# Both heads of an attention unit turned on VectorE, scores made two steps ahead, and a reordered last batch, in a fused top-k attention and feed-forward kernel

## The chip, the cores and the metric

The kernel runs on one core of a Trainium2 chip. A core has five engines that run their own instruction streams [...]: TensorE (PE in the profile, with its weight loads shown apart as PEld), VectorE (DVE), ScalarE (ACT), GpSimd (POOL) and SyncE (SP), which here only issues DMAs. The metric is device time in microseconds (us) for one whole execution; lower is better.

## The reference

Two blocks in sequence, all in float32. With batch B = 8, H = 8 heads, S = 576 rows and head width D = 64:

```
scores = (1/8) * q @ k^T                        # per batch and head, 576 x 576
kth    = 32nd largest score of each row
scores = where(scores >= kth, scores, -1e9)
attn   = exp(scores - max) / (sum + 1e-9)
x      = (attn @ v), heads side by side         # B x S x 512
xn     = (x - mean) / sqrt(var + 1e-6) * g_ln   # per row
out    = x + relu(xn @ w_ch1) @ w_ch2           # 512 -> 2048 -> 512
```

## The kernel before

**Units, groups, jobs.** The 576 query rows of a head are cut into four full blocks of 128 rows and a rest of 64. A *unit* is one block for a pair of heads: a full unit holds the two heads as two tiles of 128 x 576 scores; a rest unit packs the 64 rest rows of both heads into one tile. A *group* is a set of units of one head pair whose probabilities are multiplied with the values together (blocks 0 and 1, or 2 and 3, with the rest rows, J = 4, put with one of them). A *job* is a group's work with its loads. There are 5 units for each of 4 head pairs and 8 batches: 160 units, in `units`, batch by batch.

**The step loop** (L900) makes one pass per unit and six more. In step n it works on several units at once, and the order of the calls in the loop is the order of the instructions on every engine; nothing is rescheduled. For unit n, `select` finds the 32nd largest score on VectorE, in four parts spread over the step. For unit n+1, `scores` (L329) makes the scores on TensorE, and ScalarE copies them from PSUM to a tile `sc`. For unit n-1, `mask` (L439) forms a masked score on ScalarE; for unit n-2, called `ex`, `weigh` (L446) takes the exponential with its row sum on ScalarE, and the probabilities are turned so that keys lie on partitions. For the group that ended at unit n-3, `values` (L558) multiplies the turned probabilities, in the tile `pt`, with v. `place` turns the result back and scales it by the row sums.

**Select.** From the ninth unit on, `halve` (L363) first folds a row of 576 into its larger and its smaller halves: VectorE writes `hi` = max(a, b), and GpSimd writes `lo` = a + b, and then lo - hi, in whole numbers. `select_halved` (L381) takes the 16 largest of `lo`, puts them behind `hi`, and then takes the 32 largest of 304 by MAX8 and MATCH_REPLACE8. The first eight units use 576-wide MAX8 and MATCH_REPLACE8 on `sc` instead (L416, L423).

**Turning.** For most tiles, `turn` (L496) turns on TensorE: four 128 x 128 transposes per head (L505), one more for the ends of both heads (L538), and ScalarE copies to `pt`. From batch 2 on, units that are not a group's last and not rest units are *moved* (72 of them): `move` (L478) turns their second head with one VectorE transpose of 32 x 32 blocks into the unit's own `sc`, SyncE stores that to HBM, and four DMAs bring it back to `pt` with the blocks in place. `move` comes after the first part of `select` in the step, and that unit's second head is masked and weighed first (`order`, L914).

**Feed-forward.** When the rows of a block of two or three 128-row tiles are complete (`gives`), its work is queued in `todo`: turn x, first products ("hidden", L680, four per 128 hidden columns), second products ("project", L697). `fill`, called at eight places in a step, takes from that list as much as `slot(n)` allots, so TensorE works on it between attention instructions. `slot` spreads the list evenly over the steps up to the next block.

**Weights.** The weights come as float64; in the first steps `Piece.split`, `shift` and `join` make float32 of them on ScalarE, VectorE and GpSimd. The gain g_ln is multiplied into w_ch1 on GpSimd in `join`.

**Buffers that matter here:** `sc` has 4 tiles, `e` (masked scores, then probabilities) 2, `lo` 1, `pt` 1, five PSUM banks serve scores, turns and values, and three serve the feed-forward products.

Of the kernel before, what the change touches and what calls it, by code (L numbers as in the profile page):

```python
# [16 lines left out]
TOP_K = 32  # L17
# [12 lines left out]
def kernel(  # L30
# [66 lines left out]
    scpool = pool("sc", 4)  # L97
# [4 lines left out]
    otpool = pool("ot", 2)  # L102
# [4 lines left out]
    rpool = pool("r", 2)  # L107
# [34 lines left out]
    class Piece:  # L142
# [26 lines left out]
        def split(self):  # L169
# [5 lines left out]
            self.low = tmp("low", FP32)  # L175

            pl, tag = ((opool, "o"), (rpool, "r"))[self.i % 2]
            self.sign = pl.tile([P, DM], FP32, tag=tag, name="sign")
# [5 lines left out]
            nc.scalar.activation(self.sign[:], high, AF.Sign)  # L184
            nc.gpsimd.tensor_scalar(size_f, size_f, HIGH_MAX, HIGH_MIN, ALU.min, ALU.max)
# [6 lines left out]
        def join(self):  # L192
            size = self.size[:]
            nc.gpsimd.tensor_tensor(size, size, self.low[:].bitcast(U32), ALU.add)
            size = size.bitcast(FP32)
            if self.i < NF:
                gain = gcol[:, self.c : self.c + 1].to_broadcast([P, DM])
                nc.gpsimd.tensor_tensor(size, size, gain, ALU.mult)
            nc.gpsimd.tensor_tensor(self.dst, size, self.sign[:], ALU.mult)
            ready[self.i] = now[0]  # L200
# [107 lines left out]
    class Unit:  # L308
        def __init__(self, job, group, qt):
# [5 lines left out]

            self.halved = False
# [46 lines left out]
    def halve(u):  # L363
# [11 lines left out]
        nc.gpsimd.tensor_tensor(lo.bitcast(I32), a.bitcast(I32), b.bitcast(I32), ALU.add)  # L375
        nc.vector.tensor_tensor(hi, a, b, ALU.max)  # L376
        nc.gpsimd.tensor_tensor(  # L377
            lo.bitcast(I32), lo.bitcast(I32), hi.bitcast(I32), ALU.subtract
        )

    def select_halved(u, i):  # L381
# [24 lines left out]
    def select(u, i):  # L406

        if u.halved:
            return select_halved(u, i)
        nt = range(len(u.tiles))  # L410
        if i == 0:
            u.cur = [u.sc[:, t] for t in nt]
            u.wk = {}
        m = small.tile([P, 2, 8], FP32, tag=f"m{i}", name=f"m{i}")
        for t in nt:
            nc.vector.max(m[:, t, :], u.cur[t])  # L416
        if i < TOP_K // 8 - 1:
            for t in nt:
                if i == 0:

                    o = (NF - 4 + 2 * t) * DM
                    u.wk[t] = w2[:].rearrange("p f n -> p (f n)")[:, o : o + S]
                nc.vector.match_replace(u.wk[t], m[:, t, :], u.cur[t], LOWEST)  # L423
                u.cur[t] = u.wk[t]
        if i == 0:
            u.top = m
        u.thr = m

    def prepare(u):
# [5 lines left out]
        engine = nc.vector if u.i < CONVERTING else nc.gpsimd  # L435
        engine.tensor_tensor(b, u.thr[:, 0:nt, 7], u.top[:, 0:nt, 0], ALU.subtract)  # L436
        engine.tensor_scalar(b, b, scale, 0.0, ALU.mult, ALU.add)  # L437
# [28 lines left out]
    def place_of(u):  # L466
# [4 lines left out]
        if g.pt is None:  # L471
            g.pt = ptpool.tile([P, 2 * J + 1, GQ], FP32, tag="pt", name="pt")
            g.ptB = g.pt[:, J : 2 * J].rearrange("p c n -> p (c n)").rearrange(
                "p (i c n) -> p i c n", c=J, n=32
            )
        return sum(P for x in g.qts if x < u.qt)

    def move(u):  # L478

        i0 = place_of(u) // 32  # L480
        t = u.sc[:, 1, 0:JP]
        nc.vector.transpose(
            t.rearrange("p (j c n) -> p j c n", j=P // 32, c=J),
            u.e[:, 1, R:S].rearrange("p (c j k) -> p j c k", c=J, k=32),
        )
        hbm = hbmpool.tile([P, JP], FP32, tag="turned", name="turned")
        nc.sync.dma_start(hbm[:], t)
        for j in range(P // 32):
            nc.sync.dma_start(
                u.group.ptB[j * 32 : (j + 1) * 32, i0 : i0 + P // 32].rearrange(  # L490
                    "k i c n -> k i (c n)"
                ),
                hbm[:, j * P : (j + 1) * P].rearrange("(i k) x -> k i x", k=32),
            )

    def turn(u):  # L496

        g = u.group
        q0 = place_of(u)
        i0 = q0 // 32  # L500

        def part(t):
# [6 lines left out]
            if u.rest:  # L509
                both = ps[:].rearrange("p (c h n) -> p h c n", h=2, n=R)  # L510
                nc.scalar.copy(g.pt[:, 0:J, q0 : q0 + R], both[:, 0])
                nc.scalar.copy(
                    g.ptB[:, i0 : i0 + R // 32],
                    both[:, 1].rearrange("p c (i n) -> p i c n", n=32),
                )
            elif t == 0:
                nc.scalar.copy(  # L517
                    g.pt[:, 0:J, q0 : q0 + P], ps[:].rearrange("p (c n) -> p c n", n=P)
                )
            else:  # L520
                nc.scalar.copy(
                    g.ptB[:, i0 : i0 + P // 32],
# [18 lines left out]
        heads = [0] if u.moved else range(len(u.tiles))  # L541
# [16 lines left out]
    def values(g):  # L558
        vb = g.job.v
        av = brief("av")  # L560
        for c in range(J):
            for h in range(2):
# [3 lines left out]
                    g.ptB[:, 0 : g.nq // 32, c, :] if h else g.pt[:, c, 0 : g.nq],  # L566
# [47 lines left out]
    class Block:  # L614
# [40 lines left out]
        def items(self):  # L655
# [21 lines left out]
            def hidden(f, c):  # L677
                if c == 0:
                    ps["h"] = product("hps")
                nc.tensor.matmul(  # L680
                    ps["h"][:, 0:N],
# [5 lines left out]
                if c == NC - 1:  # L687
                    per = J // n if n in (1, 2) else 1
                    if f % per == 0:
                        hT["h"] = hpool.tile([P, J * P], FP32, tag="h", name="h")  # L690
                    hT[f] = hT["h"][:, f % per * N : (f % per + 1) * N]
                    nc.scalar.activation(hT[f], ps["h"][:, 0:N], AF.Relu)  # L692
# [363 lines left out]
```

## Time and profile before

| | |
|---|---|
| median of 3 runs | 1665.12 us (1665.03 to 1666.29) |
| the profiled execution | 1668.59 us, of which the span of its instructions 1666.8 us |
| TensorE matmul busy | 1574.1 us, 94% |
| VectorE busy | 1464.5 us, 88% |
| ScalarE busy | 1077.2 us, 65% |
| GpSimd busy | 664.0 us, 40% |
| DMA | 104.58 MB, mean 63 GB/s |

Engines overlap, so the shares do not add up to the span. A busy share is an average over the whole span; the start, the long middle and the end have different limits, and the page's slices show them apart. Float32 products appear in the trace as two matmul instructions each, transposes as one, so 576 second products of the program are 1152 in the profile. The end of a matmul is modelled; the distance from one start to the next is what a matmul takes in a run of them.

### The profile page before, as it was taken

What the parts mean: (1) busy time and instruction counts of PE and PEld (TensorE: products, weight loads), DVE (VectorE), ACT (ScalarE), POOL (GpSimd) and SP (SyncE); (2) the same over time, 40 slices, a digit from 0 to 9 for tenths busy, and PEclk for the clock granted to TensorE, in tenths of its full rate; (3) what the DMA queues carried; (4) which work ended last, traced back from release to release, by engine and by line L of the source; (5) the groups of instructions that cost most, each with busy time, mean ns of one, the idle gap of its engine ahead of it and who ended that gap; (6) DMA issues with size and microseconds to landing.
All of it is one profiled execution on the core that took longest, in us unless ns stands there. A gap on an engine that the chain in (4) does not pass through costs nothing.

```text
span 1666.8 us, 25284 instructions
## 1 busy us (share of the span) xinstructions
PE 1574.1 (94%) x7113; PEld 955.1 (57%) x7113; DVE 1464.5 (88%) x4476; ACT 1077.2 (65%) x2759; POOL 664.0 (40%) x879
## 2 busy tenths in 40 slices
PE   3568989989999999999999999999999999999998
PEld 1346556566555575755547575745547575755564
DVE  5998999999999999999999999899998999998000
ACT  5677967767666776767666675767666676665310
POOL 5567854343433434343343434343243433333010
PEclk9758999999999999999999999999999999999999
DMA  7423333001331133213231233112331132111000
GB/s 176 100 64 108 89 58 59 22 14 27 76 81 51 53 76 81 65 54 69 59 86 51 55 73 83 52 54 70 65 89 44 53 81 74 52 46 47 26 13 13
DMA packets 301203, 104.58 MB, mean 63 GB/s; under 512 B 246276, under 2 KB 283144, under 8 KB 301064
## 3 DMA queue, kind: packets, MB, share of 16 engines
q1 hardware_dynamic: 296328, 102.39, 24.4%
q10 hardware_dynamic: 4736, 0.59, 0.3%
q8 instruction: 57, 0.93, 0.2%
q14 instruction: 82, 0.67, 0.1%
HBM read 74.58 MB, written 28.31 MB: 62 GB/s over the span
## 4 chain that ended last, share of the span: by engine, by line
PE 71%; DVE 21%; issue 4%; ACT 2%; POOL 1%; DMA 1%; ACTq 0%; POOLq 0%; DVEq 0%; SPq 0%
PE hps L680 25%; PE ops L697 24%; PE scps L354 8%; PE av L563 6%; DVE m L398 5%; DVE hi L385 4%; PE tp L505 4%; DVE hi L390 2%; DVE m L416 2%; PE av L570 2%; DVE w L423 2%; DVE lo L385 1%; DVE hi L376 1%; DVE size L188 1%; PE tp L667 1%
## 5 line engine op out<-in xcount | busy, mean ns | idle before, releaser
L680 PE MATMUL hps<-xT,w 128*128 128x256 f32 (+1 forms) x2048 | 550.0, 411 | 2.7 <-ACT xT L672 2.3
L697 PE MATMUL ops<-w,h 128*128 128x512 f32 x1152 | 546.1, 599 | 0.0
L398 DVE MAX8 m<-hi 128x8 f32<-128x304 f32 x1088 | 460.7, 458 | 2.3
L680 PEld LDWEIGHTS hps<-xT,w 128*128 128x128 f32 x2048 | 372.1, 191 | 108.5 <-issue 17.3
L385 DVE MATCH_REPLACE8 hi<-m,hi 128x304 f32<-128x304 f32 x816 | 368.0, 456 | 0.0
L375 POOL TENSOR_TENSOR lo<-sc 128x576 int32<-128x576 int32 (+1 forms) x152 | 197.7, 1301 | 316.3 <-ACT sc L335 156.9
L697 PEld LDWEIGHTS ops<-w,h 128*128 128x128 f32 x1152 | 200.2, 191 | 169.9 <-issue 164.6
L377 POOL TENSOR_TENSOR lo<-lo,hi 128x576 int32<-128x576 int32 (+1 forms) x152 | 196.8, 1295 | 141.9 <-DVE hi L376 139.7
L354 PE MATMUL scps<-kT,qT 64*128 64x288 f32 (+3 forms) x1344 | 217.4, 433 | 32.4 <-DVE qT L304 20.9
L335 ACT COPY sc<-scps 128x288 f32<-128x288 f32 x576 | 199.2, 409 | 62.3 <-PE scps L354 51.0
L442 ACT ACTIVATE e<-sc,m 128x576 f32<-128x576 f32 x288 | 224.3, 779 | 9.7 <-DVE m L398 6.2
L452 ACT ACTIVATE e<-e,bias 128x576 f32<-128x576 f32 x288 | 224.6, 780 | 2.9 <-DVE bias L437 2.5
L390 DVE MAX8 hi<-lo 128x8 f32<-128x288 f32 x544 | 221.8, 443 | 2.6 <-POOL lo L377 1.5
L354 PEld LDWEIGHTS scps<-kT,qT 64*128 64x128 f32 (+1 forms) x1344 | 122.4, 181 | 146.6 <-issue 56.2
L505 PEld LDWEIGHTS tp<-ident,e 128*128 128x128 f32 x864 | 110.9, 147 | 115.9 <-ACT e L452 51.7
L505 PE MATMUL tp<-ident,e 128*128 128x128 f32 x864 | 138.1, 285 | 38.2 <-ACT e L452 37.9
L692 ACT ACTIVATE h<-hps 128x256 f32<-128x256 f32 (+1 forms) x256 | 105.9, 414 | 96.5 <-PE hps L680 93.8
L436 POOL TENSOR_TENSOR bias<-m,m 128x2 f32<-128x2 f32 (+1 forms) x143 | 27.8, 195 | 303.6 <-DVE m L398 303.6
L563 PE MATMUL av<-pt,vb 128*64 128x256 f32 (+2 forms) x1088 | 146.7, 413 | 0.0
L376 DVE TENSOR_TENSOR hi<-sc 128x576 f32<-128x576 f32 (+1 forms) x152 | 138.8, 913 | 5.5 <-ACT sc L335 5.5
L385 DVE MATCH_REPLACE8 lo<-hi,lo 128x288 f32<-128x288 f32 x272 | 118.2, 440 | 0.0
L517 ACT COPY pt<-tp 128x512 f32<-128x512 f32 x128 | 74.6, 583 | 62.1 <-PE tp L505 60.5
(79 smaller groups left out, 1295.0 us busy)
## 6 DMA issues: line engine op xcount, KB each, us to landing
turned<-sc SPq DMA_DIRECT2D x72, 256.0 KB, 2.0
pt<-turned SPq DMA_DIRECT2D x288, 64.0 KB, 2.0
vb<-in_v_dram SPq DMA_DIRECT2D x136, 128.0 KB, 2.5
raw<-in_moe_w_ch_dram SPq DMA_DIRECT2D x32, 512.0 KB, 4.0
kin<-in_k_dram SPq DMA_DIRECT2D x128, 72.0 KB, 2.5
qin<-in_q_dram SPq DMA_DIRECT2D x120, 72.0 KB, 2.5
out_dram<-o SPq DMA_DIRECT2D x32, 256.0 KB, 2.2
ends<-in_v_dram SPq DMA_DIRECT2D x136, 16.0 KB, 2.2
```

What stands on the lines that cost most here:

```text
L335: nc.scalar.copy(u.sc[:, t, s * HALF : (s + 1) * HALF], made[s][t][:, 0:HALF])
L354: nc.tensor.matmul(ps[i * R : i * R + ql, o : o + width], qT[r, q0 : q0 + ql], kT[r, k0 : k0 + width], start=True, stop=True,)
L375: nc.gpsimd.tensor_tensor(lo.bitcast(I32), a.bitcast(I32), b.bitcast(I32), ALU.add)
L385: nc.vector.match_replace(x[:, t], m[:, t, :], x[:, t], LOWEST)
L390: nc.vector.max(u.hi[:, t, o : o + 8], u.lo[:, t])
L398: nc.vector.max(m[:, t, :], u.hi[:, t])
L442: nc.scalar.activation(u.e[:, t], u.sc[:, t], AF.Prelu, bias=u.thr[:, t, 7:8], scale=-1.0, alpha=SLOPE)
L452: nc.scalar.activation(u.e[:, t], u.e[:, t], AF.Exp, bias=u.bias[:, t : t + 1], scale=-scale / SLOPE, accum_out=g.den[:, col : col + 1],)
L505: nc.tensor.transpose(ps[:, c * P : (c + 1) * P], u.e[:, t, c * P + t * R : (c + 1) * P + t * R], ident[:],)
L563: nc.tensor.matmul(av[h * D : (h + 1) * D, 0 : g.nq], vb[:, h * J + c, :], g.ptB[:, 0 : g.nq // 32, c, :] if h else g.pt[:, c, 0 : g.nq], ...
L680: nc.tensor.matmul(ps["h"][:, 0:N], w1[:, c, f * P : (f + 1) * P], xT[0][:, c, 0:N], start=(c == 0), stop=(c == NC - 1),)
L697: nc.tensor.matmul(ps[i][:], hT[f][:, i * P : (i + 1) * P], w2[:, f, :], start=(f == 0), stop=(f == NF - 1),)
```

## The change

It has these parts.

- **Turning.** A moved unit has both heads turned on VectorE (two transposes), one store of twice the size and four returning DMAs of twice the size. TensorE and ScalarE no longer turn its first head. `pt` holds both heads in blocks of 32 queries. `move` stands at the end of the step, after the last part of `select`, and the heads are masked and weighed in their natural order.
- **Scores two steps ahead.** From step 17 (`CONVERTING`) on, step n makes the scores of unit n+2 in place of n+1 (`due`). `sc` has five tiles in place of four; `ot` and `r` have one each in place of two.
- **Halving.** All units are halved, the first eight too. VectorE writes `hi` first; GpSimd then makes lo = a - hi, and lo + b.
- **Feed-forward.** For blocks of one or two tiles, the first products of four or two f share one PSUM bank, with one relu over 512 columns.
- **Last batch.** Its rest rows come first, as four groups of their own; then blocks 0 and 1, then 2 and 3. The last batch thus gives blocks of 1, 2 and 2 tiles in place of 3 and 2, and has 8 moved units in place of 12: 68 in all.
- **Weights.** The gain is multiplied into the sign on ScalarE in place of GpSimd; the sign's temporary is in another pool. The bias of the first units is one VectorE instruction per head.
- **Order in a step.** `values` stands after two fills, `stats` and the reciprocals later. `slot` shares the list out in proportion to VectorE's estimated time of each step (`pace`), not evenly.

```diff
-    scpool = pool("sc", 4)
+    scpool = pool("sc", 5)
-    otpool = pool("ot", 2)
+    otpool = pool("ot", 1)
-    rpool = pool("r", 2)
+    rpool = pool("r", 1)
...
             nc.scalar.activation(self.sign[:], high, AF.Sign)
+            if self.i < NF:
+                nc.scalar.mul(self.sign[:], self.sign[:], gcol[:, self.c : self.c + 1])
...
-            if self.i < NF:
-                gain = gcol[:, self.c : self.c + 1].to_broadcast([P, DM])
-                nc.gpsimd.tensor_tensor(size, size, gain, ALU.mult)
...
-        nc.gpsimd.tensor_tensor(lo.bitcast(I32), a.bitcast(I32), b.bitcast(I32), ALU.add)
         nc.vector.tensor_tensor(hi, a, b, ALU.max)
         nc.gpsimd.tensor_tensor(
-            lo.bitcast(I32), lo.bitcast(I32), hi.bitcast(I32), ALU.subtract
+            lo.bitcast(I32), a.bitcast(I32), hi.bitcast(I32), ALU.subtract
         )
+        nc.gpsimd.tensor_tensor(lo.bitcast(I32), lo.bitcast(I32), b.bitcast(I32), ALU.add)
...
     def move(u):
-        t = u.sc[:, 1, 0:JP]
-        nc.vector.transpose(
-            t.rearrange("p (j c n) -> p j c n", j=P // 32, c=J),
-            u.e[:, 1, R:S].rearrange("p (c j k) -> p j c k", c=J, k=32),
-        )
-        hbm = hbmpool.tile([P, JP], FP32, tag="turned", name="turned")
-        nc.sync.dma_start(hbm[:], t)
+        blocks = u.sc[:].rearrange("p t n -> p (t n)")[:, 0 : 2 * JP]
+        for t in range(2):
+            nc.vector.transpose(
+                blocks.rearrange("p (j t c n) -> p j t c n", j=ni, t=2, c=J)[:, :, t],
+                u.e[:, t, t * R : t * R + JP].rearrange("p (c j k) -> p j c k", c=J, k=32),
+            )
+        hbm = hbmpool.tile([P, 2 * JP], FP32, tag="turned", name="turned")
+        nc.sync.dma_start(hbm[:], blocks)
...
-        heads = [0] if u.moved else range(len(u.tiles))
+        heads = () if u.moved else range(len(u.tiles))
...
-                if c == 0:
+                per = J // n if n in (1, 2) else 1
+                o = f % per * N
+                if c == 0 and o == 0:
                     ps["h"] = product("hps")
...
+                if c == NC - 1 and f % per == per - 1:
+                    h = hpool.tile([P, J * P], FP32, tag="h", name="h")
...
+                    nc.scalar.activation(h[:, 0 : per * N], ps["h"][:, 0 : per * N], AF.Relu)
...
-            parts[b < 2].append(J)
+            if b == B - 1:
+                parts = [[J]] + parts
+            else:
+                parts[b < 2].append(J)
...
-    for u in units[EARLY:]:
-        u.halved = True
...
-    RESERVE = 4.0
+    RESERVE = 7.0
...
+    def due(n):
+        ahead = [n + 1] if n < CONVERTING else [n + 2]
+        if n == CONVERTING:
+            ahead = [n + 1, n + 2]
+        return [units[i] for i in ahead if i < N]
...
-        if nxt:
-            scores(nxt)
-        if g:
-            values(g)
+        for x in due(n):
+            scores(x)
         if u:
             select(u, 0)
-        if moved:
-            move(ex)
...
         fill()
+        if g:
+            values(g)
...
         if u:
             select(u, 3)
             if u.i < CONVERTING:
                 prepare(u)
+        if moved:
+            move(ex)
```

## The prediction

> **What bounds the kernel now.** I read the busy shares and the slices first, then the busy time of the long middle, the waits, the groups by shape, and the timeline of single steps.
>
> ```profile
> PE 1574.1 (94%) x7113; PEld 955.1 (57%) x7113; DVE 1464.5 (88%) x4476; ACT 1077.2 (65%) x2759; POOL 664.0 (40%) x879
> ...
> PE   3568989989999999999999999999999999999998
> PEld 1346556566555575755547575745547575755564
> DVE  5998999999999999999999999899998999998000
> ```
>
> A slice is 41.7 us. VectorE is full from the second slice on while TensorE is not, up to slice 9; then both are full; VectorE has nothing in the last three.
>
> ```profile
> 400.00:1500.00 1100.00, 1095.98 (x5004) 656.16 (x5000) 1053.08 (x3288) 735.92 (x1914) 419.09 (x598) 1.00 0.25 64
> ```
>
> Busy time between 400 and 1500 us: TensorE 99.6%, VectorE 95.7%. From some 400 us on TensorE sets the end; VectorE has 47 us to spare in 1100. In the waits, VectorE's idleness has one main name:
>
> ```profile
> DVE sc L482 <- ACT e L452: 59.4, 19, 13.4
> ```
>
> `move` waits for an exponential on ScalarE, which lags with TensorE: 19 waits, 59.4 us. Early, TensorE's first product starts at 132.30 us; before, it waits for steps paced by VectorE's select. So the early 130 us count by VectorE and the rest by TensorE.
>
> **What the Trainium skill says.** "SBUF — State Buffer" (section "SBUF: two separate sides"): a VectorE instruction with two SBUF inputs and a GpSimd instruction that reads SBUF lock each other out for the whole instruction. The trace agrees: the same `hi` takes 0.74 us alone and 1.92 us when GpSimd's L375 had begun just before.
>
> ```profile
> 913.84 0.74 DVE L376 TENSOR_TENSOR hi<-sc 128x576 f32<-128x576 f32 x1
> ...
> 922.37 1.41 POOL L375 TENSOR_TENSOR lo<-sc 128x576 int32<-128x576 int32 x1 [3.18 <-ACT sc L335]
> 922.47 1.92 DVE L376 TENSOR_TENSOR hi<-sc 128x576 f32<-128x576 f32 x1
> ```
>
> "DMA: Bandwidth & Descriptors" (section "Anatomy of one DMA — SWDGE (gpsimd) path") gives some 2 us fixed for a DMA through GpSimd; these go through SyncE, and still the page's section 6 shows 2.0 us for the 256 KB store and for the 64 KB returns.
>
> **The change, part by part.** Durations are of the profiled execution: span 1666.8 us, 1668.6 us as timed, the median 1665.1; I add on the span and take off 1.7 us at the end.
>
> *TensorE.* The programs' counts of L505 go from 864 to 608: 256 turns fewer (68 moved units without 8 turns, before 72 without 4). Their price is the start-to-start distance:
>
> ```profile
> 147.63 0.60 PE L505 MATMUL tp<-ident,e 128*128 128x128 f32 x4
> 148.07 1.25 PE L680 MATMUL hps<-xT,w 128*128 128x256 f32 x5
> ```
>
> Four take 0.44 us, so 256/4 x 0.44 = **-28.2 us** where TensorE is full. (The mean of 285 ns overlaps its neighbours.) ScalarE loses 64 copies of 0.58 us, hidden.
>
> The last batch's block of 3 tiles becomes 2 and 1. 64 products of 384 columns (2 x 0.323 us) become 64 of 256 (2 x 0.216) and 64 of 128. No row shows 128 columns: by columns 2 x 0.108, no loss; if the weight load's 191 ns binds, 2 x 0.191, +10.6 us. I take the middle, **+5**. Four value products for rest rows alone are about 1 us each (the first batch has them), less some 0.5 us for each narrowed group: **+2**.
>
> *VectorE.* Transposes go from 72 to 136: 64 x 0.698 = +44.7 us. `hi` now runs before GpSimd's two instructions, no longer during the first: 120 x (1.038 - 0.745) = -35 us. In the early units, by start-to-start distances in the timeline up to 125 us, a pair of 576-wide MAX8 takes 1.33 us and a pair of replaces 1.44, so 4 x 1.33 + 3 x 1.44 = 9.6; the halved way is 0.67 (`hi`) + 2 x 0.73 (MAX8 of `lo`) + 0.85 (its replaces) + 4 x 0.75 + 3 x 0.88 (MAX8 and replaces of `hi`) = 8.6. With some 0.5 us off the bias, -1.5 x 8 = -12 us. VectorE's sum is about -2, and the 59.4 us of waiting at `move` have a step's length more of cover.
>
> *Early.* Of those 12 us I keep **-8** for the start: the first select waits for `lo`, some 3.5 us (0.75 + 2 x 1.4) at one time; ScalarE gets 16 more activations of 0.68 us, 11 us, in a stretch where it is 76% busy (38.17 of 50 us), covered unless its step outgrows VectorE's; GpSimd loses 16 x 1.04 us and gains 8 x 2.8. Bounds: -16 (with most of the contention before 400 us, 4 us, added) and +4 (ScalarE takes over the pace).
>
> *`lo` later.* It is ready 2 x 1.43 = 2.9 us after `hi`, 1.4 later than now. Between stand select's parts 2 and 3, 1.6 + 2.4 us, so it is hidden in a full step. In a rest step they are 2.0 us with 1.4 of `move`: nothing to 0.9 us in 32 steps, absorbed by VectorE's slack. Both GpSimd instructions now wait for `hi`; behind them in GpSimd's queue stand the centring of x, the residual sum and the next bias, which TensorE's turn of x and ScalarE's exponential need a step or more later. Ahead of them stands at times a residual sum (1.29 us) that waits for the last second product; if TensorE lags far, that holds `lo`, and VectorE waits for TensorE there in place of at `move`.
>
> *`move` at the end of the step.* SyncE issues as many DMAs per unit. 512 KB stores: with 102 MB taking 24.4% of 16 engines' span, 256 KB more is about 1 us of all engines, so 2.0 to 3.0 us to land; total DMA share at most some 8 points more. On SyncE's queue `move` now stands behind the loads of heads and values; the values need `pt` more than a step later, so nothing. `sc` matters: in step n the copies of scores n+2 take the tile of unit n-3, which `move` read at the end of step n-1. Two transposes 1.4 us, issue 0.35, landing 2.1: free 3.8 us after that step's select ends. Queued behind that wait on ScalarE are relu, exponential and copies, and TensorE for their banks. I take **0**, since TensorE has a fill or two, the values and three product banks to go on with, and a constant lag is paid once. Below zero is not excluded: idle before VectorE's waits could shorten.
>
> *Hidden edits.* One relu per bank spares ScalarE instructions, and it idles 364 of the 1100 us; if its first product per bank now comes later, two other banks of the three cover 8 x 0.216 = 1.7 us each. `slot` and the later `values` move work between steps, 0 while TensorE is full. `ot` with one tile: its reader comes in the same step, and the next group a step later at least. In the last batch four head loads come in four steps; the first load of all took 4.4 us (2.32 to 6.75 in the chain), a step 5 or more: 0, at most 2 us three times, within VectorE's slack.
>
> Sum: 1666.8 - 28.2 + 5 + 2 - 8 = 1637.6 span, less 1.7: **1636 us**.
>
> Can VectorE keep up? After its last select at about 1536 TensorE had backlog until 1604. The least behind it is the last block (1604.67 to the end, 62 us) plus a drain of some 15 (masks and exponentials 3.5, turn 2, values and copies 5, statistics and centring 2, a fill). Its last select may end as late as 1638 - 77 = 1561. From 392 on it needs 1088 + 45 - 31 = 1102 of the 1169 us: 67 us of idleness are free.
>
> **Rivals.**
>
> *VectorE becomes the bound.* In a rest step (5 us of select) `move` needs the exponential, which came 4.6 us after the step's start before (913.64 against 909.00); with ScalarE lagging 3 us, VectorE waits about 2.5 us, 20 times, 50 us; with 0.9 x 32 for `lo`, 79. That passes the 67 by 12, and coupling may double it: 1648 to 1660, say 1654. For it: both engines are over 95% busy. Against: `pace` gives rest steps less TensorE work.
>
> *Slower: the `sc` wait holds TensorE.* Its scores at 909.00 and VectorE's next select (L390 at 909.26) start together now; so aligned, each of 68 moved units would hold ScalarE some 3 us. It decides once more than 31/68 = 0.45 us of each reaches TensorE; at 1 us: 1636 + 68 = 1704. Against: VectorE leads in those 19 waits, and a lag once taken covers the wait.
>
> *The gain is spent early or in the tail.* If the start gains nothing and 128-wide products cost +10.6: 1636 + 8 + 6 = 1650.
>
> *Better:* early -16, the narrow block free, and 1100 to 1500 stays full: 1636 - 8 - 5 - some = 1620.
>
> **How the numbers follow.** Within 0.2% (1661.8 to 1668.4) is what a measurement can hardly tell from no change. Likeliest, 1624 to 1648: 0.55. Better, under 1624: 0.12. VectorE bound or gain spent, 1648 to 1662: 0.17. About the same: 0.05. Slower, the `sc` wait: 0.11. The range 1618 to 1662 leaves out the slower case, half of the same, and the best few in a hundred. Faster 0.84, same 0.05, slower 0.11.
>
> **What would show it.** L505's successor x608; `hi` at a mean near 0.75 us; VectorE at 96% in the middle with TensorE still over 99%; the first product before 128 us; the wait of the transposes in `move` well under 59 us. Wrong: TensorE's scores or turns waiting on ScalarE's copies to `sc` by tens of us; VectorE waiting on GpSimd's `lo`; first products of 128 columns at 0.19 us each.

## The result and the profile after

The changed kernel takes **1674.64 us** (median of 4 runs, 1672.19 to 1675.20) against 1665.17 us before (1665.03 to 1666.29): a ratio of the means of 1.0053, 95% interval 1.0035 to 1.0070. It is slower by about half a per cent; the forecast was 1636 us with a range of 1618 to 1662. The profiled execution of the changed kernel took 1674.27 us, its span 1672.5 us.

The page of the changed kernel, busy time and slices (41.8 us each):

```profile
PE 1569.3 (94%) x7057; PEld 941.9 (56%) x7057; DVE 1469.6 (88%) x4611; ACT 1038.1 (62%) x2615; POOL 670.7 (40%) x881
...
PE   2568989989799999999999999999999999999998
...
DVE  5997999999989999999999999999889887988600
```

TensorE's busy sum fell by only 4.8 us where 28 us of turns went. There is a new dent, a 7 in slice 11 (418 to 460 us). The long middle of the changed kernel (columns: stretch, length, then busy time of TensorE, its weight loads, VectorE, ScalarE and GpSimd, the clock, the DMA share and GB/s):

```profile
400.00:1500.00 1100.00, 1083.99 (x4788) 630.90 (x4787) 1034.25 (x3252) 672.71 (x1743) 411.81 (x587) 1.00 0.34 92
```

TensorE idles 16 us of these 1100, before 4. VectorE is not fuller than before (1034 against 1053). The groups by shape, changed kernel:

```profile
L375 DVE TENSOR_TENSOR hi<-sc 128x576 f32<-128x576 f32 x128 | 99.1, 774 | 19.5 <-ACT sc L335 19.5
L468 DVE STREAM_TRANSPOSE sc<-e 128x512 f32<-128x512 f32 x136 | 89.5, 688 | 42.1 <-ACT e L436 42.0
L490 PE MATMUL tp<-ident,e 128*128 128x128 f32 x608 | 96.8, 284 | 26.4 <-ACT e L436 25.5
L193 DVE TENSOR_SCALAR size<-size 128x512 uint32<-128x512 uint32 x32 | 30.7, 997 | 0.0
```

The 256 turns are gone (x608), `hi` has a mean of 774 ns in place of 1038, the second transposes are there. The last line is a surprise, taken up at the end. The waits of the changed kernel (total us, times, longest):

```profile
DVE sc L468 <- ACT e L436: 42.0, 20, 6.9
DVE hi L391 <- POOL lo L379: 34.2, 17, 7.5
...
DVE hi L375 <- ACT sc L335: 21.4, 9, 7.2
...
ACT sign L187 <- POOL w L201: 15.0, 7, 2.9
...
ACT sc L335 <- DMA turned<-sc: 10.7, 4, 4.9
```

`move` waits less than before (59.4 us then). VectorE's wait for `lo` was 1.5 us, once, before. Its longest in the changed kernel, with GpSimd's instructions ahead of it (a square bracket is the idle time before the instruction and what ended it):

```profile
1392.18 1.27 POOL L693 TENSOR_TENSOR o<-o,x 128x512 f32<-128x512 f32 x1 [16.78 <-ACT o L689]
1393.41 0.79 POOL L376 TENSOR_TENSOR lo<-sc,hi 128x288 int32<-128x288 int32 x1
...
1395.12 0.46 DVE L391 MAX8 hi<-lo 128x8 f32<-128x288 f32 x1 [7.53 <-POOL lo L379]
```

A residual sum on GpSimd has waited for ScalarE's `o`, which follows TensorE's last second product, and `lo` stands behind it. Nine of the 17 waits, 26.6 of the 34.2 us, follow such a held sum. ScalarE's wait for GpSimd's `w` at `sign`, 6.0 us in 3 times before, is 15.0 us in 7. The last line is the `sc` wait of the slower rival: 10.7 us in 4 times, not 68 times 3 us. DMA issues and their landing, changed kernel:

```profile
turned<-sc SPq DMA_DIRECT2D x68, 512.0 KB, 2.6
pt<-turned SPq DMA_DIRECT2D x272, 128.0 KB, 2.9
```

Both were 2.0 us at half the size before; the forecast had 2.0 to 3.0 for the store.

**Where the time went.** Busy sums hide it, since the ends of matmuls are modelled. So I took TensorE apart by distances from start to start. Runs of instructions of one kind in the traces give a pace: 0.216 us for a matmul instruction of a product of 256 columns (others by columns), 0.109 for a transpose, 1.17 for a full unit's eight score instructions, 0.117 for a value product of 256 columns. Instructions times pace is *work*; what the distance to the next group has beyond that is a *gap*. Work, gaps and 40.8 us (before the first matmul and the last run, alike in all) make the span. The rows below "after" are experiments told in the next section.

| us | span | work | gaps 0-130 | 130-250 | 250-400 | from 400 on |
|---|---|---|---|---|---|---|
| before | 1666.8 | 1475.6 | 92.3 | 16.6 | 17.5 | 24.0 |
| after | 1672.5 | 1448.6 | 90.6 | 22.9 | 17.6 | 52.1 |
| before_three_signs | 1674.6 | 1475.6 | 91.3 | 26.7 | 16.8 | 23.7 |
| sign_four | 1662.1 | 1448.6 | 89.9 | 13.6 | 17.8 | 51.3 |
| first_head_on_TensorE | 1692.2 | 1478.2 | 89.0 | 22.9 | 17.5 | 43.6 |
| values_first | 1677.0 | 1448.6 | 93.0 | 29.5 | 20.9 | 44.0 |
| late_values_early_only | 1652.7 | 1448.6 | 89.5 | 11.3 | 20.3 | 42.0 |
| last_batch_as_before | 1663.9 | 1444.2 | 89.7 | 21.8 | 17.3 | 50.1 |
| scores_one_ahead | 1678.0 | 1448.6 | 88.5 | 24.2 | 17.5 | 58.3 |
| even_slots | 1665.6 | 1448.6 | 88.8 | 22.9 | 16.6 | 47.8 |
| mended_not_halved | 1646.8 | 1444.2 | 87.8 | 11.3 | 20.1 | 42.7 |

Work fell by 27.0 us, close to the forecast's part of it. Gaps grew by 32.8: 28.1 from 400 us on, where I had reckoned with none, and 6.3 between 130 and 250 us. One gap stands out on TensorE's timeline of the changed kernel:

```profile
447.83 1.10 PE L354 MATMUL scps<-kT,qT 64*128 64x288 f32 x6
455.67 1.12 PE L648 MATMUL tp<-ident,r 128*128 128x128 f32 x4 [6.74 <-POOL r L619]
```

TensorE waits 6.74 us for the centred rest rows; before, its longest wait between 400 and 520 us was 2.18 us. I took the late statistics of these rows for the cause, which experiment 3 does not bear out. The other gaps are small and many. Some 12 of the 28 us are in gaps under 0.2 us each, where TensorE goes from one kind of product to another: by the paces above 26.1 us in 920 such changes from 400 us on, against 13.8 us in 1020 before. These are, for the most part, too short to be listed as waits for another engine.

### The profile page after: what moved, and what is told of

It reads as the page before. It is cut to its first block, busy times and chain, and to the rows that moved or that the text cites. A ratio compares the mean times of both kernels' runs of the same rounds, so it can differ in the third digit from the quotient of the medians.

```text
span 1672.5 us, 24921 instructions
## 1 busy us (share of the span) xinstructions
PE 1569.3 (94%) x7057; PEld 941.9 (56%) x7057; DVE 1469.6 (88%) x4611; ACT 1038.1 (62%) x2615; POOL 670.7 (40%) x881
## 3 DMA queue, kind: packets, MB, share of 16 engines
q1 hardware_dynamic: 298312, 137.12, 30.7%
## 4 chain that ended last, share of the span: by engine, by line
PE 63%; DVE 23%; ACT 5%; issue 4%; POOL 3%; DMA 1%; SPq 0%; ACTq 0%; POOLq 0%; DVEq 0%
PE hps L664 23%; PE ops L680 21%; PE scps L354 7%; DVE m L399 7%; DVE hi L386 6%; PE av L544 6%; DVE hi L391 3%; DVE lo L386 2%; PE tp L490 2%; PE av L551 2%; DVE hi L375 2%; DVE size L193 1%; POOL lo L376 1%; POOL lo L379 1%; ACT e L426 1%
## 5 line engine op out<-in xcount | busy, mean ns | idle before, releaser
L664 PE MATMUL hps<-xT,w 128*128 128x256 f32 (+2 forms) x2176 | 551.6, 398 | 3.9 <-ACT xT L653 3.9
L399 DVE MAX8 m<-hi 128x8 f32<-128x304 f32 x1152 | 489.2, 461 | 3.3
L376 POOL TENSOR_TENSOR lo<-sc,hi 128x576 int32<-128x576 int32 (+1 forms) x160 | 208.4, 1303 | 478.8 <-DVE hi L375 276.1
L391 DVE MAX8 hi<-lo 128x8 f32<-128x288 f32 x576 | 234.5, 444 | 35.3 <-POOL lo L379 34.2
L379 POOL TENSOR_TENSOR lo<-lo,sc 128x576 int32<-128x576 int32 (+1 forms) x160 | 207.2, 1295 | 12.5
L675 ACT ACTIVATE h<-hps 128x512 f32<-128x512 f32 (+1 forms) x156 | 88.3, 566 | 99.8 <-PE hps L664 98.8
L375 DVE TENSOR_TENSOR hi<-sc 128x576 f32<-128x576 f32 (+1 forms) x160 | 114.0, 712 | 21.4 <-ACT sc L335 21.4
L693 POOL TENSOR_TENSOR o<-o,x 128x512 f32<-128x512 f32 x32 | 41.0, 1280 | 225.2 <-ACT o L689 225.2
L468 DVE STREAM_TRANSPOSE sc<-e 128x512 f32<-128x512 f32 x136 | 89.5, 688 | 42.1 <-ACT e L436 42.0
L490 PE MATMUL tp<-ident,e 128*128 128x128 f32 x608 | 96.8, 284 | 26.4 <-ACT e L436 25.5
L490 PEld LDWEIGHTS tp<-ident,e 128*128 128x128 f32 x608 | 77.3, 147 | 75.2 <-ACT e L436 37.7
```

Of the source, the lines that this page charges most:

```text
L376: nc.gpsimd.tensor_tensor(lo.bitcast(I32), a.bitcast(I32), hi.bitcast(I32), ALU.subtract)
L379: nc.gpsimd.tensor_tensor(lo.bitcast(I32), lo.bitcast(I32), b.bitcast(I32), ALU.add)
L391: nc.vector.max(u.hi[:, t, o : o + 8], u.lo[:, t])
L399: nc.vector.max(m[:, t, :], u.hi[:, t])
L490: nc.tensor.transpose(ps[:, c * P : (c + 1) * P], u.e[:, t, c * P + t * R : (c + 1) * P + t * R], ident[:],)
L664: nc.tensor.matmul(ps["h"][:, o : o + N], w1[:, c, f * P : (f + 1) * P], xT[0][:, c, 0:N], start=(c == 0), stop=(c == NC - 1),)
```

## The experiments

Each run's ratio is to the kernel before in its own series (medians 1666.45 to 1666.78 us), so I compare ratios and give a difference as ratio times 1666 us; with the intervals combined such a difference is good to some 3 to 4 us. Edits are on the changed kernel unless said, and are shown shortened to the lines that matter. In the recorded texts A is my theory for that run, and R, R', S or S' its rivals.

**1. The sign's temporary.** The change cut the `r` pool from two tiles to one to pay for the fifth `sc`. Its second tile also held a sign of the weight conversion: signs went round four tiles, two of `o` and two of `r`. In the changed kernel those of the first weight are in the hidden pool, and those of the second go round three, two of `o` and one of `r`. A fourth tile is given back, in a piece of `w2` that isn't yet written:

```
-  pl, tag = ((opool, "o"), (opool, "o"), (rpool, "r"))[self.i % 3]
+  pl, tag = ((opool, "o"), (opool, "o"), (rpool, "r"), (None, None))[self.i % 4]
+  if pl is None:
+      self.sign = w2[:, NF - 1, :]
```

> The changed kernel with four temporaries for the sign of the second weights again, in place of three; the fourth lies in the unwritten last part of those weights. Theory A: ScalarE's six waits of 2 to 3 us for GpSimd's join between 150 and 215 us go, and with them VectorE's for the scores, so the stretch up to 230 us becomes some 5 us shorter: about 1669 us. Rival R': other buffers take over the wait, or the start does not count: 1673 to 1676 us.

Measured: 1663.12 us, 0.9982 [0.9973, 0.9991], that is 11.8 us better than the changed kernel, more than expected. The opposite, the kernel before with only this one edit of the change:

```
-  rpool = pool("r", 2)
+  rpool = pool("r", 1)
-  pl, tag = ((opool, "o"), (rpool, "r"))[self.i % 2]
+  if self.i < NF: self.sign = tmp("sign", FP32)
+  else: pl, tag = ((opool, "o"), (opool, "o"), (rpool, "r"))[self.i % 3]
```

> The kernel before with one thing changed: the sign temporaries as in the changed kernel (three for the second weights, from the two output tiles and one row tile; the first weights' in the hidden pool). Theory A (three temporaries hold ScalarE between 150 and 215 us, whatever else is in the kernel): some 8 to 12 us slower than before, 1674 to 1679 us. Rival R' (it hurts only together with the halving of the first units, which fills GpSimd): 1665 to 1670 us.

Measured: 1678.17 us, 1.0065 [1.0050, 1.0080]: 10.8 us slower than before, by this edit alone. Undone it gives what done alone it costs, so the cause is shown. (This edit also leaves the rows one `r` tile; the fourth sign tile does not give that back, so what the two runs share is the ring of the signs.) How it works, by ScalarE on the timeline of the changed kernel, and TensorE with it:

```profile
163.34 0.67 ACT L187 ACTIVATE sign<-raw 128x512 f32<-128x512 f32 x1 [2.63 <-POOL w L201]
...
164.40 0.77 ACT L426 ACTIVATE e<-sc,m 128x576 f32<-128x576 f32 x1
...
165.06 0.57 ACT L502 COPY pt<-tp 128x512 f32<-128x512 f32 x1
...
165.69 0.75 PE L354 MATMUL scps<-kT,qT 64*128 64x288 f32 x2 [1.84 <-ACT pt L502]
```

The sign may be written only when GpSimd has multiplied the sign of three pieces earlier. It waits 2.63 us at the head of ScalarE's stream; the mask and the copy to `pt` stand behind it, and TensorE's scores behind the copy's bank. The same wait in the kernel before, in the changed kernel with the fourth tile, and in the kernel before with three:

```profile
ACT sign L184 <- POOL w L199: 6.0, 3, 3.9
```

```profile
ACT sign L190 <- POOL w L204: 0.7, 1, 0.7
```

```profile
ACT sign L187 <- POOL w L202: 15.8, 7, 2.8
```

And the stretch from 130 to 250 us: before, after, with the fourth tile, and the kernel before with three.

```profile
130.00:250.00 120.00, 112.54 (x573) 73.33 (x572) 113.90 (x338) 94.54 (x235) 86.35 (x88) 0.94 0.32 82
```

```profile
130.00:250.00 120.00, 109.67 (x526) 69.58 (x525) 105.34 (x313) 89.00 (x213) 81.83 (x83) 0.93 0.30 77
```

```profile
130.00:250.00 120.00, 113.72 (x594) 75.01 (x594) 111.68 (x343) 95.53 (x231) 87.58 (x90) 0.96 0.33 82
```

```profile
130.00:250.00 120.00, 105.27 (x508) 66.52 (x507) 107.84 (x306) 88.13 (x218) 81.46 (x83) 0.92 0.28 75
```

All engines do less in the same time when the ring has three tiles: 526 and 508 matmuls against 573 and 594. Seven waits of some 2 us are 15 us of waiting, and some 11 us reach the end.

**2. The turning itself.** The first head goes back to TensorE, and everything else of the change stays; `move` turns, stores and returns only the second:

```
-  for t in range(2):
+  for t in (1,):
-  heads = () if u.moved else range(len(u.tiles))
+  heads = (0,) if u.moved else range(len(u.tiles))
```

> The changed kernel with the first head of the 68 moved units turned on TensorE again (four turns and a copy each, and half the moved data), all else as changed. Theory A (after some 456 us TensorE is full and sets the end): 68 x 4 turns of 0.109 us come back, +29.7 us, less a few us of waits for the larger moves: 1695 to 1704 us. Rival R (VectorE, which loses 68 transposes of 0.69 us = 47 us, sets the pace): 1640 to 1674 us.

Measured: 1693.75 us, 1.0166 [1.0149, 1.0183]. So the turning on VectorE is worth 18.8 us in the changed kernel: it is the gain that it was taken for, though not all of 29.6. By the table it takes 29.6 us of work away and leaves 8.5 more of gaps from 400 us on. From 700 to 1100 us, the changed kernel and this one:

```profile
700.00:1100.00 400.00, 397.11 (x1749) 232.37 (x1746) 393.20 (x1237) 250.09 (x653) 155.16 (x218) 1.00 0.37 100
```

```profile
700.00:1100.00 400.00, 399.51 (x1831) 240.41 (x1829) 369.37 (x1183) 261.25 (x670) 149.27 (x214) 1.00 0.27 65
```

With both heads moved VectorE is 98.3% full there and TensorE 99.3%; with one, 92.3% and 99.9%. The two are near balance, and each now waits a little for the other.

**3. The order in a step.** First `values` back to its old place, right after the scores:

```
     scores(x)
+    if g: values(g)
 ...
     fill()
-    if g: values(g)
```

> The changed kernel with the value products put back directly after the scores in a step. Theory A (TensorE is still the bound, and its 27 us of saved turns went into gaps of its own, made by the new order in the step): the gaps at the changes from and to the value products, +14 us against the kernel before by the start-to-start distances after 400 us, go away: 1674.6 - 14 = about 1661 us. Rival R (VectorE now sets the pace, TensorE only waits for it wherever it stands): the order of TensorE's work makes no difference, 1672 to 1677 us.

Measured: 1677.71 us, 1.0067 [1.0052, 1.0082], no gain. I was wrong on the whole, yet the table shows two effects: gaps from 400 us on fall by 8.1, and before 400 they grow by 12.3. Why they grow before 400 us was not parted further. From 400 us on the gaps under 0.2 us fall to 15.0 us in 910 changes, but a new wait comes in. TensorE on this kernel's timeline:

```profile
467.88 4.53 PE L544 MATMUL av<-pt,vb 128*64 128x320 f32 x16 [6.91 <-DMA pt<-turned]
```

The value products now stand ahead of TensorE's other work of the step and wait there for the returning DMA, 12.3 us in three waits.

Then `stats` alone, back from behind the third part of `select` to before the last weights:

```
         load(fresh[later], nc.sync, nc.sync)
+    for blk, i in rows_of.pop(n, []): blk.stats(i)
 ...
     select(u, 2)
-    for blk, i in rows_of.pop(n, []): blk.stats(i)
```

> The changed kernel with the row statistics put back ahead of the third part of select. Theory A: the one wait of TensorE for the centred rest rows near 449 us (6.7 us) and some shorter ones go: about 1667 us. Rival R: no difference, 1672 to 1677 us.

Measured: 1671.80 us, 1.0034 [1.0021, 1.0047]: 3.2 us, not told from nothing. The wait that I had put down to the late statistics is still there, 0.9 us shorter, and the gaps from 400 us on fall by only half a microsecond:

```profile
452.75 1.11 PE L648 MATMUL tp<-ident,r 128*128 128x128 f32 x4 [5.85 <-POOL r L619]
```

And these two with the fourth sign tile:

> The changed kernel with all three put back: value products first, statistics early, four sign temporaries. Theory A: the gains add, 1674.6 - 14 - 7 - 5 = about 1648 us, faster than the kernel before by 1 per cent. Rival R: 1665 to 1675 us.

Measured: 1664.07 us, 0.9986 [0.9978, 0.9995], the same as the sign tile alone. Against that run the gaps fall by 7.9 us from 400 us on, where I had counted on 14 and 7, and grow by 9.7 before. So the two effects of `values` were parted: late in the steps up to 17, where weights are still converted, early after them.

```
     scores(x)
+    if g and n > CONVERTING: values(g)
 ...
     fill()
-    if g: values(g)
+    if g and n <= CONVERTING: values(g)
```

> The changed kernel with four sign temporaries, statistics early, and the value products directly after the scores from step 18 on, but after two fills up to step 17. Theory A: 1663.1 (four sign temporaries) - 2.8 (statistics, from its own run) - 8 (gaps of TensorE after 400 us with the value products first, 43.4 against 51.3 us): about 1652 us, faster than the kernel before by 0.8 per cent. If the place of the value products matters only in sum with the start: 1660 us.

Measured (with the fourth tile and `stats` early): 1655.10 us, 0.9930 [0.9915, 0.9945]. Against the fourth tile alone the two order edits give 8.7 us, and gaps from 400 us on fall from 51.3 to 42.0. As `stats` alone took half a microsecond off these gaps, most of it should be the place of the value products. It is a sum of two: the gaps under 0.2 us fall from 25.8 to 15.0 us, and TensorE has waits for the returned DMA that it did not have with late values:

```profile
PE av L547 <- DMA pt<-turned: 12.4, 3, 6.8
```

The longest of them, 6.8 us at 444 us, stands where the wait for the rest rows stood. One of the two, 4.8 to 7.7 us long, is there in every variant of the changed kernel that was run, so which part of the change makes this hole is not shown.

**4. The last batch.** Only its order is put back (blocks of 3 and 2 tiles, 72 moved units):

```
-  if b == B - 1:
-      parts = [[J]] + parts
-  else:
-      parts[b < 2].append(J)
+  parts[b < 2].append(J)
```

> The changed kernel with the last batch in its old order (rest rows with blocks 0 and 1; 72 moved units; a block of 3 tiles and one of 2). Theory A: TensorE's work falls by 16 turns (1.8 us) and the four value products of their own (2 us), and it is full to the end in either order: 1668 to 1674 us. Rival R: VectorE ends later relative to TensorE and the tail after its last select grows by a tile's 28 us of products: 1685 to 1700 us.

Measured: 1666.01 us, 0.9995 [0.9986, 1.0004]: 9.7 us better than the changed kernel. The same edit on the kernel of experiment 3:

> The best version so far (four sign temporaries, statistics early, value products after two fills only up to step 17) with the last batch in its old order as well. If the gains add: 1655.1 - 8.6 = about 1646.5 us, 1.2 per cent faster than the kernel before, which would be the turns' 27 us less some 8. If the two overlap: 1650 to 1655 us.

Measured: 1649.18 us, 0.9895 [0.9880, 0.9910], 5.8 us better than without it. The new last batch costs 6 to 10. Of it, 4.4 us is TensorE work: 3.5 of that is the 32 turns (0.109 each; I had expected 16) of the four units that aren't moved any more, 0.3 the narrow products, 0.5 the values. The gaps from 1400 us on are 8.2 us with it and 4.7 without, but over all from 400 us on only 2.0 less without. The narrow products on TensorE's timeline of the changed kernel:

```profile
1495.19 0.83 PE L664 MATMUL hps<-xT,w 128*128 128x128 f32 x6
1495.86 0.27 PE L519 MATMUL tp<-ident,e 128*128 128x128 f32 x1
```

Six start in 0.67 us, 0.112 each: no loss to the weight load.

**5. Halving.** GpSimd's sum first again, as before the change:

```
+  nc.gpsimd.tensor_tensor(lo.bitcast(I32), a.bitcast(I32), b.bitcast(I32), ALU.add)
   nc.vector.tensor_tensor(hi, a, b, ALU.max)
-  nc.gpsimd.tensor_tensor(lo.bitcast(I32), a.bitcast(I32), hi.bitcast(I32), ALU.subtract)
-  nc.gpsimd.tensor_tensor(lo.bitcast(I32), lo.bitcast(I32), b.bitcast(I32), ALU.add)
+  nc.gpsimd.tensor_tensor(lo.bitcast(I32), lo.bitcast(I32), hi.bitcast(I32), ALU.subtract)
```

> The changed kernel with the old order of the halving: GpSimd's a + b, VectorE's larger half, GpSimd's subtraction. VectorE's larger half is then held up by GpSimd again, some 0.3 us in each full unit, 38 us in all. Theory A: up to 456 us VectorE sets the pace, so 40 units x 0.2 to 0.3 us = +8 to +12 us there, nothing later: 1680 to 1687 us. Rival R: most of the 38 us: 1700 to 1712 us.

Measured: 1678.55 us, 1.0072 [1.0057, 1.0087]: 3.2 us slower, at the edge of what can be told. Its group of `hi`:

```profile
L376 DVE TENSOR_TENSOR hi<-sc 128x576 f32<-128x576 f32 x128 | 110.7, 865 | 17.2 <-ACT sc L335 17.2
```

The mean rises from 774 to 865 ns, VectorE's busy sum from 1469.6 to 1485.5. The new order is a small gain at best. Then the first eight units whole, as before (their old 576-wide select, not printed here, comes back with this):

```
-  if nxt:
+  if nxt and nxt.i >= EARLY:
       halve(nxt)
```

> The changed kernel with the first eight units selected on whole rows, as before. Theory A (up to 456 us VectorE sets the pace): 1.0 us more of VectorE in each of eight steps, less GpSimd's 23 us and the wait for the first smaller half: +3 to +8 us, 1678 to 1683 us. Rival R' (ScalarE and GpSimd already pace the first steps): 1671 to 1676 us.

Measured: 1672.18 us, 1.0031 [1.0020, 1.0042]. I had expected a loss of 3 to 8 us; it is 3.7 better, so the early halving brings no gain.

**6. Two steps ahead, relu per bank, the uneven spread.**

```
-  ahead = [n + 1] if n < CONVERTING else [n + 2]
-  if n == CONVERTING:
-      ahead = [n + 1, n + 2]
+  ahead = [n + 1]
```

> The changed kernel with the scores of unit n+1 made in step n throughout, five tiles as changed. Theory A: TensorE is full after some 456 us; the four waits of ScalarE for the moved scores (10.7 us) go and VectorE waits a little more: 1670 to 1678 us. Rival R: the distance is what keeps VectorE fed; its larger half waits for ScalarE's copies, and TensorE starves: over 1685 us.

Measured: 1680.39 us, 1.0082 [1.0065, 1.0099], 4.8 us slower. Making the scores two steps ahead spares VectorE waits for ScalarE's copies; with one step they are:

```profile
DVE hi L375 <- ACT sc L335: 89.3, 56, 7.7
```

It was 21.4 us in 9 times with two ahead. One relu for each first product:

```
-  o = f % per * N
-  if c == 0 and o == 0: ps["h"] = product("hps")
+  o = 0
+  if c == 0: ps["h"] = product("hps")
```

> The changed kernel with one bank and one relu for each first product, as before. Theory A: ScalarE has room, the banks too: 1673 to 1677 us. Rival S (a bank held over two products stalls TensorE): 1665 to 1671 us. Rival S' (ScalarE's 96 saved relus feed the turns sooner): 1679 to 1685 us.

Measured: 1672.90 us, 1.0037 [1.0023, 1.0052]: no difference that can be told. The spread of feed-forward work even again:

```
-  RESERVE = 7.0
+  RESERVE = 4.0
-  ratio = min(ratio, (left - RESERVE + pe) / dve)
-  return max(0.0, ratio * pace(n) - pe_cost(n)) / SLOTS
+  even = min(even, (left - RESERVE) / (m - n))
+  return max(0.0, even) / SLOTS
```

> The changed kernel with the feed-forward work spread evenly over the steps again and a reserve of 4. Theory A (TensorE full in the middle whatever the spread; its small gaps of 1 to 2 us per 50 us are of the order in a step): 1671 to 1679 us. Rival S (the uneven spread itself leaves TensorE without work at some steps, and is the rest of the loss): 1662 to 1668 us. Rival S' (it is what lets VectorE keep up): over 1682 us.

Measured: 1666.61 us, 1.0000 [0.9991, 1.0008]: 8.8 us better, in the range of rival S. But that isn't a cost that the spread has in every kernel, as the last pair shows.

**7. The parts that pay, kept.** Fourth sign tile, `stats` early, `values` late up to step 17 only, last batch as before, first eight units whole; both heads on VectorE, two steps ahead, `hi` first and the uneven spread stay.

> The best version (four sign temporaries, statistics early, value products late only up to step 17, the last batch in its old order) with the first eight units on whole rows as well: 1649.2 - 2.5 = about 1647 us if that gain adds; 1649 to 1652 us if four sign temporaries had already given it.

Measured: **1647.86 us, 0.9884 [0.9867, 0.9900]**, better than both kernels. The page, and the long middle:

```profile
PE 1548.3 (94%) x6825; PEld 927.7 (56%) x6825; DVE 1467.9 (89%) x4547; ACT 1032.0 (63%) x2607; POOL 645.9 (39%) x863
```

```profile
400.00:1500.00 1100.00, 1080.75 (x4739) 636.55 (x4738) 1075.63 (x3387) 688.18 (x1786) 422.10 (x602) 0.99 0.36 99
```

VectorE is busy 97.8% of the middle, against 94.0% in the changed kernel; from 1100 to 1400 us the changed kernel has it busy for 261 of 300 us, and with only the last batch put back (experiment 4) for 293. The same kernel with the even spread:

> The best version (four sign temporaries, statistics early, value products late only up to step 17, the last batch in its old order, the first eight units on whole rows) with the even spread of the feed-forward work as well: 1647.9 - 8.0 = about 1640 us if that gain adds; 1646 to 1650 us if the other repairs had already given it.

Measured: 1655.85 us, 0.9932 [0.9916, 0.9949]: here the even spread is 8.0 us *worse*. Its sign depends on the rest of the change. One wait of TensorE goes with it, that of the first products for ScalarE's copies of the turned x: 9.9 us in 4 times with the even spread, 2.6 in 2 with the uneven one. In the changed kernel it is 6.0 us in 3 times with the even spread and 3.9 in 2 with the uneven one.

**The sum of the parts.** Costs, each found by undoing it: sign tile 11.8, last batch 9.7, spread 8.8, order 8.7, early halving 3.7, relu 2.7. Gains: turning 18.8, two ahead 4.8, `hi` first 3.2. That makes +18.6 against the 8.8 (0.0053 x 1666) measured. (The 8.7 was found with the fourth sign tile in; 3.7, 2.7 and 3.2 are no more than a difference is good to.) The parts aren't additive: the sign tile, the order, the last batch and the early halving, all undone, give 28.2 us together where they sum to 33.9, and the spread changes sign. No run undid `move` at the end of the step, the order of the heads, the gain on ScalarE, the bias in one instruction, the later reciprocals or the single `ot` tile. So how the missing 10 us divide between interplay, these parts and noise is open, and so is why the even spread helps the changed kernel.

## Why the prediction was wrong

Two steps failed above all. The sum let TensorE stay full from 400 us on, with 0 for the new order in a step; its gaps there grew by 28.1 us. And it had no term for the shorter ring of the signs, which costs 11.8 us.

- **"From some 400 us on TensorE sets the end."** True before the change. After it, TensorE and VectorE are close to even from 700 to 1100 us, and gaps from 400 us on took up as much as the turns had freed. Two signs that I had named were missed: between 400 and 1500 us VectorE is at 94.0%, not 96, and TensorE at 98.5%, not over 99.
- **The turns, -28.2.** The mechanism was right and its work was measured (27.9 for the transposes in the start-to-start account, net of all turns), but the part is worth 18.8 where undoing it brings back 29.6 of work. The term is right only for an engine that stays full; with VectorE at 98% from 700 to 1100 us, some 9 us of it came back as gaps.
- **The narrow block +5, values +2.** They measured 0.3 and 0.5 of work. I took the middle of two bounds, and the lower, by columns, held. The last batch as a whole I had at +7 beside its 3.5 of turns, and it costs 6 to 10 with them: near, but by luck, as what it costs beyond 4.4 us of work is in no term.
- **VectorE's sum, -2.** Its parts came close: `hi` by 120 x (1038 - 774 ns) = -32 us where I had -35, and the transposes by 89.5 - 50.3 = +39 us where I had +45. The whole is +5; the slower shift, 32 x (997 - 590 ns) = 13 us, was not in the sum. The `lo` wait I had named as a sign of being wrong, and the held residual sum as a way to it, but without a price; it is 34.2 us. Some 20 of these lie after 1100 us; from there to 1400 us TensorE is busy for 298 of 300 us and VectorE for 261, so they are not what sets the end there.
- **"Early -8".** The failed step of the start. Gaps to 130 us shrank by 1.7 and the first product came 4.2 us earlier (128.13 us, just short of the sign "before 128"), but the halving of the first eight units, from which two thirds of the 12 us had come, is not needed for it: without it the first product starts at 126.84 us. And by 250 us the sign tile had taken more than that back. That run's 1672.18 us lies in the range of its rival, that ScalarE and GpSimd already pace the first steps; no run tests this further.
- **`sc` wait 0.** Right: 10.7 us of it in 4 waits, where the slower rival needed 0.45 us in each of 68.
- **"`slot` and the later `values` move work between steps, 0 while TensorE is full."** This is the step that failed most: it takes as given what it had to show. `values` and `stats` late cost 8.7 us together (late `values` up to step 17 only is the better choice), by small gaps at the changes between kinds of products more than by waits; the spread costs 8.8 or -8.0 as the rest goes.
- **What had no term at all.** The `r` pool "one tile in place of two" stood in my own description of the change, and I followed only `ot` to its readers. Its second user, the sign, was worth 11.8 us, the largest single cost, alone more than the whole loss. With it mended the changed kernel is at 0.9982 of the kernel before.
- **The rivals.** "VectorE becomes the bound" (1654) has the closeness of the two engines right, and its waits came near: 42.0 us in 20 times at `move` for its 50 in 20, 34.2 for `lo` for its 29. But all but 2.6 of the 42.0 lie after 1100 us, where VectorE has idle time to spare (261 of 300 us busy up to 1400), so they are not shown to set the end. "Slower by the `sc` wait" gave the right side for the wrong reason. "The gain is spent early or in the tail" had the start right and the 128-wide products wrong. None held an added wait in the weight conversion.

The gains alone, each as measured, would give 1667 - 19 (turns) - 5 (two ahead) - 3 (`hi`) = 1640. The best kernel that was run, 1647.86 us, reaches 19 of these 27 us. Four parts, the sign tile, the order, the spread and the last batch, cost 9 to 12 us each as undone; I had put three of them at nothing or without a term.

## What to carry to other kernels

A tile taken from one pool to pay for another is a change of its own: follow its tag to every user, since a ring one tile shorter puts a wait at the head of an in-order stream, and all that is queued behind pays. Removing work from a full engine pays only while it stays full: here 27.0 us less work came with 32.8 us more of gaps. So write down which work will fill the hole at each place of the step, count the changes between kinds of products too, and account for work and gaps apart, by distances from start to start. When a change has many parts, undo them one at a time before judging any: here a losing change held a gain of 1.2%.

## What the runs showed of the hardware

- VectorE's shift of the weight conversion (one SBUF input) took 590 ns in the mean before, 997 after, 813 with the first eight units not halved, at the same size and count; only the work around it had changed. The row of the kernel before, then one shift of it with nothing on GpSimd, and one of the changed kernel with GpSimd's instruction that had begun just before:

```profile
L188 DVE TENSOR_SCALAR size<-size 128x512 uint32<-128x512 uint32 x32 | 17.8, 590 | 7.3 <-POOL size L185 7.3
```

```profile
96.83 0.42 DVE L188 TENSOR_SCALAR size<-size 128x512 uint32<-128x512 uint32 x1
```

```profile
126.57 1.57 POOL L376 TENSOR_TENSOR lo<-sc,hi 128x576 int32<-128x576 int32 x1
126.80 1.63 DVE L193 TENSOR_SCALAR size<-size 128x512 uint32<-128x512 uint32 x1
```

  In the changed kernel 12 of the 32 shifts take 1.48 us or more, in the kernel before 2; each of the 14 starts 0.11 to 0.24 us after a GpSimd instruction and ends 0.27 to 0.29 us after that one's end. The six before with nothing on GpSimd take 0.39 to 0.43 us. Not every overlap holds the shift: five in the kernel before start 0.1 us after GpSimd's L377 and still take 0.42 us.

  The Trainium skill, "SBUF — State Buffer" (section "SBUF: two separate sides"), names VectorE instructions in a two-port mode as sharing the lock with GpSimd, beside those with two inputs. The held shifts fit it; that this shift runs in such a mode no trace here shows.
- Float32 products of 128 columns kept the pace of 0.112 us for each matmul instruction, though a weight load in the trace has a mean of 191 ns: as recorded, successive loads must overlap.
- DMAs of twice the size landed in 2.6 (store) and 2.9 us (returns) in place of 2.0, with the main queue's share of the engines' span at 30.7% in place of 24.4%. The size is not all of it: in experiment 2 the store of 256 KB, which writes every second piece of the doubled layout, took 2.6 us too, and the returns of 64 KB 2.0.
